# Sums of v on sixteen 32x32 TensorE tiles in four PSUM banks, with dense matmuls moved around each visit, and x and the first weights in larger packets

## The chip, the core and the metric

The kernel runs on one core of one Trainium2 chip. The metric is device time in microseconds of one launch, from the first to the last instruction and what lies around them. A profile is one execution of its own, with its own time beside the span of its instructions.

## What is computed

The reference mixes two branches of a layer over 2048 rows of 512 numbers with a gate per row:

```python
x = A_x
g = _sigmoid((x * gate_w).sum(-1, keepdims=True))
a = jnp.einsum("bsd,ed->bse", x, dft_hid_re);  b = jnp.einsum("bsd,ed->bse", x, dft_hid_im)
A = jnp.einsum("ts,bse->bte", dft_seq_re, a) - jnp.einsum("ts,bse->bte", dft_seq_im, b)
qkv = x @ wqkv                       # 32 heads of 16
scores = q @ k.T * 16 ** -0.5        # each query sees its last 256 keys
B = softmax(scores) @ v @ wo
return g * A + (1 - g) * B
```

Everything is in float32. Nearly all of the arithmetic is in the two 2048x2048 products of the first branch ("the sequence DFT" below); the second branch is a windowed attention.

## The kernel before

**Two streams on one TensorE.** The attention is a loop over 8 groups of four heads times 16 blocks of 128 rows (`n` from 0 to 127, `k = n - 9` for the part that lags behind), in four steps `p` each. The other stream is a Python generator, `dense()`, which emits one dense matmul at each `next`: the projections to q, k and v, the hidden DFT, and after those the sequence DFT (`c_block`, `c_pair`). When the last projection has been emitted, `"proj"` is put into the set `have`. `fill` runs twice in each step `p` and takes 1.95 items of the dense stream each time. Every dense product is made of three float32r terms of split operands (hi times hi, hi times lo, lo times hi); the splitting is done by `hi_of` (ScalarE) and `lo_of` (VectorE or GpSimd).

**A dense item while attention runs** is a pair of matmuls (`mm`, L218): the upper 64 rows of the operands go into one PSUM bank, the lower 64 rows into another, and the two run side by side in the array. "Pair" below means this.

**A step of the attention.** `s_head` (L337) makes a block of scores in PSUM; VectorE reduces it over the keys to the row's bound (L340, a custom operation on tile `sm` with its accumulator read into `nm`). `t_head` (L394) makes the transposed scores of an older block with that bound folded in; ScalarE takes the exponential into the SBUF tile `pt` (L395), and GpSimd zeroes what lies outside the window (L401, L405). Once in four blocks, `m_rows` (L347, L348 and four transposes, L352, all VectorE) turns sixteen columns of bounds into rows for a later block.

**A visit of `pv`.** Once in four blocks, in step `p == 2` between its two `fill` calls, `pv(u)` multiplies the exponentials with v: for each of 4 or 6 blocks of keys (`kb`; 4 when `u` is a multiple of 4), four heads `j` and two halves `h` of 64 rows, one float32 matmul of a 64x32 weight tile of `vpad`, which streams up to 320 columns of `pt`. The two halves add into two PSUM tiles `o`, the four heads into four groups of 32 partitions of each. TensorE then holds eight independent 64x32 tiles. The profile shows a float32 matmul as two passes, so a visit of 6 blocks is 48 instructions and 96 rows. Column 16 of `vpad` is ones, so the sums of the exponentials come along. ScalarE copies the first tile to `os` (L426), VectorE adds the second (L427), and `o_out` stores `os`. There are 32 visits.

**PSUM.** Of the eight banks, four belong to the dense sums. The other four (`ps_a`, tag `st`) are taken in rotation by `s`, `t` and `o` tiles alike. A tile can be written when the operation that reads the bank's former tile is done.

**Order.** Nothing is rearranged after the Python code has run: each engine executes its instructions in the order of the calls. `defer(ticks, fn)` puts a call off by a number of ticks of a clock that each dense item and each step moves on; `tick(9)` after `pv` runs what is due in the next nine.

**The start.** `load_x_first(0)` loads the first quarter of x in four transfers of 128x512 on SyncE's queue and the first q and k weights come in four of 128x256 on ScalarE's (L144). `first_w(dk)` and two more calls split one quarter of the weights and of x at a time; `qk_first` multiplies them, quarter 0 unsplit.

Of the kernel before, what the change touches and what calls it, by code (L numbers as in the profile page):

```python
# [35 lines left out]
def fnet_window_mix(ctx: ExitStack, tc: tile.TileContext, xT, x, wqk, wv, wr, wi, cr, ci, wo, gw, out):  # L36
# [40 lines left out]
    def ld(dst, src):  # L77
        nc.sync.dma_start(dst, src)
# [50 lines left out]
    def load_x_first(ss):  # L129
        for j in range(2):  # L130
            raw = pt_tile([P, 1024])
            for c in range(2):
                XRAW[2 * j + c, ss] = raw[:, HALVES[c]]
            if ss:
                ld(raw.rearrange("p (k s) -> p k s", k=2), xT[ss, 2 * j:2 * j + 2].rearrange("k p s -> p k s"))
# [272 lines left out]
    def pv(u, last=False):  # L408
        g, sb = divmod(u, 4)
        ot = [ps_a.tile([P, 512], F32, name="o", tag="st") for _ in range(2)]  # L410
        kbs = range(max(0, 4 * sb - 2), 4 * sb + 4)
        for kb in kbs:
            pt = PT[g * NB + kb]
            v2 = V2[g * 4 + kb // 4][:, kb % 4]
            for j in range(NH):
                for h in range(2):
                    r = slice(64 * h, 64 * h + 64)
                    a = max(kb * P + (64 * h if kb else 0), sb * 512)
                    e = min(kb * P + 64 * h + 320, sb * 512 + 512)
                    nc.tensor.matmul(ot[h][32 * j:32 * j + 32, a - sb * 512:e - sb * 512], v2[r, j],  # L420
                                     pt[r, j, a - kb * P:e - kb * P], start=kb == kbs[0], stop=kb == kbs[-1],
                                     skip_group_check=True)
# [3 lines left out]
        nc.scalar.copy(os, ot[0])  # L426
        defer(3, lambda: nc.vector.tensor_add(os, ot[1], os))  # L427
        hf = g // 4
# [8 lines left out]
        def o_pack():  # L437
            rows_ = us.rearrange("g j r s -> (g j) r s")
            ld(ls[0], rows_[:, 16])
            ld(o_scr[sb][2 * hf:2 * hf + 2].rearrange("a (b d) s -> (a b) d s", d=16), rows_[:, 0:16])  # L440
            defer(d, l_in)
# [303 lines left out]
    def ring_ahead(n):  # L745
        nonlocal loaded
        while loaded < 4 * NS:
# [6 lines left out]
            loaded += 1  # L754

    def fill(n):
        nonlocal quota
# [18 lines left out]
    for n in range(N + LAG + 1):  # L776
# [4 lines left out]
        for p in range(NH):  # L781
# [71 lines left out]
```

## Time and profile before

| | |
|---|---|
| median of 3 runs | 800.89 us (799.94 to 800.99) |
| the profiled execution | 799.78 us, span of its instructions 798.1 us |
| granted TensorE clock, mean | 0.999 |
| busy share of the span | PE 99%, PEld 87%, DVE 63%, ACT 55%, POOL 53% |
| chain that ended last | PE 98%; the L218 matmuls alone 64%, L420 9% |
| L420 (`pv`) | 2816 matmul rows, 74.0 us busy, at 91 us to 699 us of the span |

PE is TensorE's matmuls, PEld its weight loads, DVE VectorE, ACT ScalarE, POOL GpSimd, SP SyncE. In the views, a row has the start and the length in us, the engine, the source line, the operation, the tile written and the tiles read, the shape, the count, and in brackets the idle time of the engine just before and what ended it. Matmuls are pipelined: their rows overlap, and the distance between two starts says more than a row's length.

### The profile page before, as it was taken

The numbers are of one execution on the slowest core, as the hardware profiler recorded it, in microseconds if no ns is written. First come the engines' busy times: TensorE is split into PE (matmuls) and PEld (weight loads), VectorE is DVE, ScalarE is ACT, GpSimd is POOL, SyncE is SP. The second block draws the span as 40 slices with busy tenths as digits, with TensorE's granted clock in tenths as the row PEclk, the third lists the DMA queues.
The fourth block names the chain that finished last, engine by engine and source line by source line (L and its number), as shares of the span: only waits on it lengthen the run. The fifth ranks groups of instructions, "written<-read, shape, count | busy, mean of one in ns | idle before, by whom it ended". The sixth has DMA issues, their size and how long they took to land.

```text
span 798.1 us, 22896 instructions
## 1 busy us (share of the span) xinstructions
PE 792.8 (99%) x8716; PEld 691.6 (87%) x8716; DVE 502.9 (63%) x1529; ACT 436.6 (55%) x892; POOL 421.0 (53%) x690
## 2 busy tenths in 40 slices
PE   9999999999999999999999999999999999999998
PEld 6788899989998998899888888998899988888886
DVE  5388888887887665656665655566756671255542
ACT  6334776667767665655556556565655555422210
POOL 5002666666667676666566666665765667500000
PEclk9999999999999999999999999999999999999999
DMA  7866778886785256657666554997756545578872
GB/s 287 264 170 210 226 258 278 269 275 210 238 259 183 62 150 199 195 147 224 196 168 177 168 139 145 261 295 229 228 171 192 160 151 172 167 244 264 290 224 80
DMA packets 87438, 164.06 MB, mean 206 GB/s; under 512 B 29504, under 2 KB 31456, under 8 KB 87200
## 3 DMA queue, kind: packets, MB, share of 16 engines
q1 hardware_dynamic: 85888, 160.49, 66.0%
q10 hardware_dynamic: 1440, 2.10, 0.7%
q8 instruction: 69, 1.13, 0.7%
q14 instruction: 41, 0.34, 0.2%
HBM read 109.84 MB, written 57.16 MB: 209 GB/s over the span
## 4 chain that ended last, share of the span: by engine, by line
PE 98%; DVE 1%; issue 0%; POOL 0%; POOLq 0%
PE d L218 64%; PE d L214 9%; PE o L420 9%; PE t L214 5%; PE t L394 5%; PE s L337 5%; PE t L127 0%; DVE sm L340 0%; DVE mhl L348 0%; DVE mt L352 0%; DVE mhl L347 0%; DVE lo L87 0%; DVE ev L729 0%; DVE es L226 0%; POOL mask L124 0%
## 5 line engine op out<-in xcount | busy, mean ns | idle before, releaser
L218 PE MATMUL d<-big,hi 64*128 64x512 f32 x2096 | 364.5, 393 | 0.0
L340 DVE CUSTOM_DVE_ANT_0 sm<-s,mask 128x384 f32<-128x384 f32 (+2 forms) x512 | 271.2, 530 | 136.6 <-PE s L337 76.9
L395 ACT ACTIVATE pt<-t 128x384 f32<-128x384 f32 (+2 forms) x512 | 238.2, 471 | 155.9 <-PE t L394 81.6
L218 PEld LDWEIGHTS d<-big,hi 64*128 64x128 f32 x2096 | 218.0, 186 | 21.1 <-issue 1.1
L218 PE MATMUL d<-big,lo 64*128 64x512 f32 x1048 | 223.3, 392 | 0.0
L401 POOL TENSOR_SCALAR_AFFINE_SELECT pt<-pt 128x256 f32<-128x256 f32 x256 | 107.7, 421 | 166.5 <-ACT pt L395 147.9
L87 POOL TENSOR_TENSOR lo<-raw,hi 128x512 fp32r<-128x512 f32 x120 | 155.2, 1304 | 25.8 <-ACT hi L84 25.4
L337 PE MATMUL s<-ring,ring 48*128 48x384 f32 (+2 forms) x512 | 162.6, 326 | 0.3
L394 PE MATMUL t<-ring,ring 50*128 50x384 f32 (+2 forms) x512 | 162.1, 328 | 0.0
L218 PEld LDWEIGHTS d<-big,lo 64*128 64x128 f32 x1048 | 115.0, 186 | 10.5 <-issue 0.2
L218 PE MATMUL d<-hi,big 64*128 64x512 f32 x656 | 119.7, 392 | 0.0
L337 PEld LDWEIGHTS s<-ring,ring 48*128 48x128 f32 x512 | 92.1, 184 | 9.7 <-DVE nm L340 2.2
L394 PEld LDWEIGHTS t<-ring,ring 50*128 50x128 f32 x512 | 91.0, 184 | 6.8 <-DVE nm L340 0.7
L405 POOL TENSOR_SCALAR_AFFINE_SELECT pt<-pt 128x256 f32<-128x256 f32 x224 | 92.9, 415 | 0.0
L84 ACT CAST hi<-raw 128x512 fp32r<-128x512 f32 x146 | 87.5, 616 | 8.5 <-issue 7.6
L87 POOL TENSOR_TENSOR hl<-es,hl 128x512 fp32r<-128x512 f32 x34 | 46.1, 1355 | 72.9 <-ACT hl L84 67.0
L218 PEld LDWEIGHTS d<-hi,big 64*128 64x128 f32 x656 | 75.9, 186 | 6.6 <-DVE es L226 0.4
L420 PEld LDWEIGHTS o<-pt,vpad 64*32 64x32 f32 x2816 | 60.2, 106 | 18.5 <-issue 6.1
L218 PE MATMUL d<-lo,big 64*128 64x512 f32 x328 | 75.8, 393 | 0.0
L420 PE MATMUL o<-pt,vpad 64*32 64x320 f32 (+5 forms) x2816 | 74.0, 348 | 0.0
L223 ACT ACTIVATE es<-d 128x512 f32<-128x512 f32 x69 | 41.3, 598 | 26.0 <-PE d L218 22.9
L426 ACT COPY os<-o 128x512 f32<-128x512 f32 x32 | 18.8, 586 | 64.4 <-PE o L420 64.4
(75 smaller groups left out, 783.2 us busy)
## 6 DMA issues: line engine op xcount, KB each, us to landing
qk_scr<-hl SPq DMA_DIRECT2D x32, 512.0 KB
ring<-qk_scr SPq DMA_DIRECT2D x128, 128.0 KB
raw<-cr SPq DMA_DIRECT2D x32, 512.0 KB
raw<-ci SPq DMA_DIRECT2D x32, 512.0 KB
ab_scr<-hl SPq DMA_DIRECT2D x20, 512.0 KB
big<-ab_scr SPq DMA_DIRECT2D x17, 512.0 KB
ring<-qk_scr SPq DMA_DIRECT2D x128, 64.0 KB
u_scr<-os SPq DMA_DIRECT2D x32, 256.0 KB
```

The lines of the kernel that those rows point to most:

```text
L84: nc.scalar.copy(hi, raw)
L87: (nc.gpsimd if pool else nc.vector).tensor_sub(lo, raw, f(hi))
L214: nc.tensor.matmul(pss[0], w, x, start=start, stop=stop)
L218: nc.tensor.matmul(pss[h], w[r], x[r], start=start, stop=stop)
L223: nc.scalar.activation(t, pss[0], AF.Copy, scale=scale)
L337: nc.tensor.matmul(ps[:, :w], ring[0][r, p, jb * P:(jb + 1) * P], ring[1][r, p, k0:k0 + w], start=True, stop=True)
L340: nc.vector.tensor_tensor_reduce(out=sm[:, :w], in0=ps[:, :w], in1=mask[:, WIN - w:], scale=1.0, scalar=3e38, op0=OP.add, op1=OP.min, accu ...
L394: nc.tensor.matmul(ps[:, :w], ring[1][r, p, q0:q0 + P], ring[0][r, p, q0:q0 + w], start=True, stop=True)
L395: nc.scalar.activation(pt[:, j, :w], ps[:, :w], AF.Exp, scale=-1.0)
L401: nc.gpsimd.affine_select(a, a, pattern=[[0, 2], [1, P]], compare_op=OP.is_ge, fill=0.0, base=0, channel_multiplier=-1)
L405: nc.gpsimd.affine_select(a, a, pattern=[[0, 2], [-1, P]], compare_op=OP.is_gt, fill=0.0, base=0, channel_multiplier=1)
L420: nc.tensor.matmul(ot[h][32 * j:32 * j + 32, a - sb * 512:e - sb * 512], v2[r, j], pt[r, j, a - kb * P:e - kb * P], start=kb == kbs[0], st ...
```

## The change

Three edits.

**Sixteen tiles.** Once `"proj"` is in `have`, `pv` cuts the 128 rows into four parts of 32 instead of two of 64. Each part streams 288 columns at most instead of 320, into an `o` tile of its own, so a visit takes four PSUM tiles and 96 instructions (64 when there are 4 blocks) instead of two tiles and 48 (32). ScalarE copies the first tile, and VectorE adds three instead of one, each into `os`; the store follows 16 ticks after instead of 7. In the built program this holds for the last 22 of the 32 visits: 17 of 6 blocks and 5 of 4.

**Dense items moved.** Around such a visit `borrow` takes three items of the dense stream just ahead of `pv` and five just behind it. `fill` pays the eight back over the next 32 calls, a quarter of an item each, so that it takes 1.7 in a call in place of 1.95. The number of dense matmuls is the same (4664 at L218 and L214, counting each of a pair).

**Larger packets.** The host lays x out so that two quarters of the contraction stand side by side: the first x comes in two transfers of 128x1024 instead of four of 128x512 (and the others contiguous), the first weights in two of 128x512 instead of four of 128x256.

```diff
     def load_x_first(ss):
...
-            if ss:
-                ld(raw.rearrange("p (k s) -> p k s", k=2), xT[ss, 2 * j:2 * j + 2].rearrange("k p s -> p k s"))
-            else:
-                for c in range(2):
-                    ld(raw[:, HALVES[c]], xT[ss, 2 * j + c])
+            ld(raw, xT[ss, j])
...
-    for dk in range(DK):
-        c = slice(dk * 256, dk * 256 + 256)
+    for c in HALVES:
         nc.scalar.dma_start(wqraw[:, c], wqk[0][:, c])
...
     def pv(u, last=False):
-        ot = [ps_a.tile([P, 512], F32, name="o", tag="st") for _ in range(2)]
+        rows_ = 32 if "proj" in have else 64
+        ot = [ps_a.tile([P, 512], F32, name="o", tag="st") for _ in range(P // rows_)]
...
-                for h in range(2):
-                    r = slice(64 * h, 64 * h + 64)
-                    a = max(kb * P + (64 * h if kb else 0), sb * 512)
-                    e = min(kb * P + 64 * h + 320, sb * 512 + 512)
+                for h in range(P // rows_):
+                    r = slice(rows_ * h, rows_ * h + rows_)
+                    a = max(kb * P + (rows_ * h if kb else 0), sb * 512)
+                    e = min(kb * P + rows_ * h + 256 + rows_, sb * 512 + 512)
...
         nc.scalar.copy(os, ot[0])
-        defer(3, lambda: nc.vector.tensor_add(os, ot[1], os))
+        for h in range(1, P // rows_):
+            defer(3 * h, nc.vector.tensor_add, os, ot[h], os)
...
-        defer(7, o_out)
+        defer(7 if rows_ == 64 else 16, o_out)
...
+    def borrow(n):
+        nonlocal debt
+        debt += n
+        for _ in range(n):
+            next(stream, None)
     def fill(n):
...
-        quota += rate / 2
+        pay = min(debt, 0.25)
+        debt -= pay
+        quota += rate / 2 - pay
...
+                    wide = "proj" in have
+                    if wide:
+                        borrow(3)
                     pv(k // 4 - 1)
                     tick(9)
+                    if wide:
+                        borrow(5)
                     v_ahead(k // 4 + 1)
```

Lines of the kernel after stand a few lines off: L213 is the pair of L218, L332 and L389 the heads of L337 and L394, L416 the matmul of L420, L335 the reduction of L340, L342 to L347 those of `m_rows`, L75 the adds of L427 (they are called from `tick`).

TensorE's order at the twentieth visit (464 us in the trace of before), from the last `t` head ahead of it to the first matmuls of `pv`. Names are tiles (`d` the dense sums), the sizes those of the moving operand, and the brackets the engines whose semaphores the instruction waits for. Before:

```order
L394 MATMUL t<-ring_261,ring_262 128x384 [waits Activation_49]
L218 MATMUL d_8414<-big,hi 128x512
L218 MATMUL d_8415<-big,hi 128x512
L218 MATMUL d_8414<-big,lo 128x512
L218 MATMUL d_8415<-big,lo 128x512
L420 MATMUL o<-pt,vpad_271 32x64 [waits DVE_49]
L420 MATMUL o<-pt,vpad_271 32x128 [waits Activation_49]
L420 MATMUL o<-pt,vpad_271 32x64
```

Two pairs stand between, and the two `o` tiles wait for the readers of the two banks taken longest ago. The same place after:

```order
L389 MATMUL t<-ring_257,ring_258 128x384 [waits Activation_49]
L213 MATMUL d_8831<-big,lo 128x512
L213 MATMUL d_8832<-big,lo 128x512
L213 MATMUL d_8831<-big,hi 128x512
L213 MATMUL d_8832<-big,hi 128x512
L213 MATMUL d_8831<-big,hi 128x512
L213 MATMUL d_8832<-big,hi 128x512
L213 MATMUL d_8831<-big,lo 128x512 [waits Pool_49]
L213 MATMUL d_8832<-big,lo 128x512
L416 MATMUL o<-pt,vpad_267 32x32 [waits DVE_49]
L416 MATMUL o<-pt,vpad_267 32x64 [waits Activation_49]
L416 MATMUL o<-pt,vpad_267 32x96 [waits DVE_49]
```

Now four pairs stand between (five at other visits), and the third matmul of `pv` waits for VectorE a second time: it writes the bank of the `s` tile made in this same step.

VectorE's order there, from the reduction of step `p == 1` to the add behind the visit. Before:

```order
L340 ISA sm,nm<-s,mask 128x384 [waits DVE_49,PE_49]
L340 ISA nm 128x1
L347 TENSOR_SCALAR mhl<-nm 128x16
L348 SCALAR_TENSOR_TENSOR mhl<-nm,mhl 128x16 [waits DVE_49]
L352 STREAM_TRANSPOSE mt<-mhl 32x32 [waits DMAHW5_49,DVE_49]
L352 STREAM_TRANSPOSE mt<-mhl 32x32 x3
L340 ISA sm,nm<-s,mask 128x384 [waits PE_49]
L340 ISA nm 128x1
L427 TENSOR_TENSOR os<-o,os 128x512 [waits DMAHW7_49,PE_49,Activation_49]
L340 ISA sm,nm<-s,mask 128x384 [waits PE_49]
```

And after:

```order
L335 ISA sm,nm<-s,mask 128x384 [waits DVE_49,PE_49]
L335 ISA nm 128x1
L342 TENSOR_SCALAR mhl<-nm 128x16
L343 SCALAR_TENSOR_TENSOR mhl<-nm,mhl 128x16 [waits DVE_49]
L347 STREAM_TRANSPOSE mt<-mhl 32x32 [waits DMAHW1_49,DVE_49]
L347 STREAM_TRANSPOSE mt<-mhl 32x32 x3
L335 ISA sm,nm<-s,mask 128x384 [waits PE_49]
L335 ISA nm 128x1
L75 TENSOR_TENSOR os<-o,os 128x512 [waits DMAHW6_49,PE_49,Activation_49]
L75 TENSOR_TENSOR os<-o,os 128x512 [waits DVE_49,PE_49] x2
L335 ISA sm,nm<-s,mask 128x384 [waits PE_49]
```

In both, `m_rows` stands between the reductions of steps 1 and 2; after, three adds in place of one stand ahead of the reduction of step 3. On TensorE seven pairs (six at some visits) follow the visit before the heads of step 3, in place of two, and then three or four in each step in place of four.

More of the change, by code (lines that the diff above doesn't have):

```diff
@@ L133, in load_x_first @@
                 XRAW[2 * j + c, ss] = raw[:, HALVES[c]]
-            if ss:
-                ld(raw.rearrange("p (k s) -> p k s", k=2), xT[ss, 2 * j:2 * j + 2].rearrange("k p s -> p k s"))
-            else:
-                for c in range(2):
-                    ld(raw[:, HALVES[c]], xT[ss, 2 * j + c])
+            ld(raw, xT[ss, j])
     wqraw = pt_tile([P, 1024])
     wq0 = [st.tile([P, 1024], F32R, name=h) for h in ("hi", "lo")]
-    for dk in range(DK):
-        c = slice(dk * 256, dk * 256 + 256)
+    for c in HALVES:
         nc.scalar.dma_start(wqraw[:, c], wqk[0][:, c])
@@ L437, in o_pack @@
         def o_pack():
-            rows_ = us.rearrange("g j r s -> (g j) r s")
-            ld(ls[0], rows_[:, 16])
-            ld(o_scr[sb][2 * hf:2 * hf + 2].rearrange("a (b d) s -> (a b) d s", d=16), rows_[:, 0:16])
+            ur = us.rearrange("g j r s -> (g j) r s")
+            ld(ls[0], ur[:, 16])
+            ld(o_scr[sb][2 * hf:2 * hf + 2].rearrange("a (b d) s -> (a b) d s", d=16), ur[:, 0:16])
             defer(d, l_in)
@@ L754, in ring_ahead @@
             loaded += 1
+    debt = 0.0
+    def borrow(n):
[3 more added lines that the diff above has]
+            next(stream, None)
     def fill(n):
-        nonlocal quota
+        nonlocal quota, debt
         rate = FILL_FIRST if n < LAG else FILL_SEQ if "proj" in have else FILL_PROJ
-        quota += rate / 2
+        pay = min(debt, 0.25)
+        debt -= pay
+        quota += rate / 2 - pay
         while quota >= 1:
@@ L832 @@
     arrays = {
-        "xT": x.T.reshape(DK, P, 4, 512).transpose(2, 0, 1, 3),
+        "xT": x.T.reshape(2, 2, P, 4, 512).transpose(3, 0, 2, 1, 4).reshape(4, 2, P, 1024),
         "x": x.reshape(16, P, D),
```

## The prediction

> **What bounds the kernel now.** The page comes first: which engine is full, and which engine the last chain runs through.
>
> ```profile
> span 798.1 us, 22896 instructions
> PE 792.8 (99%) x8716; PEld 691.6 (87%) x8716; DVE 502.9 (63%) x1529; ACT 436.6 (55%) x892; POOL 421.0 (53%) x690
> PE 98%; DVE 1%; issue 0%; POOL 0%; POOLq 0%
> PE d L218 64%; PE d L214 9%; PE o L420 9%; PE t L214 5%; PE t L394 5%; PE s L337 5%; PE t L127 0%; DVE sm L340 0%; DVE mhl L348 0%; DVE mt L352 0%; DVE mhl L347 0%; DVE lo L87 0%; DVE ev L729 0%; DVE es L226 0%; POOL mask L124 0%
> ```
>
> TensorE is the bound from end to end. Whatever shortens its matmuls is gained in full, and whatever makes it wait is lost in full. The number of dense matmuls does not change, so moving them costs nothing by itself, but neither can they hide a wait: each is used once. Next, the chain in order of time gives the length of a visit of `pv`, here one of 6 blocks and the next one of 4:
>
> ```profile
> 464.00 0.47 PE d L218 x4
> 464.47 2.32 PE o L420 x65
> 466.80 0.68 PE d L218 x4
> ...
> 484.43 1.88 PE o L420 x54
> ```
>
> Then the timeline of that first visit, which is one of the 22 that change (u = 19). TensorE:
>
> ```profile
> 462.56 0.34 PE L394 MATMUL t<-ring,ring 50*128 50x384 f32 x1
> 462.57 0.34 PE L337 MATMUL s<-ring,ring 48*128 48x384 f32 x1
> 462.74 0.63 PE L218 MATMUL d<-big,hi 64*128 64x512 f32 x4
> 463.21 0.39 PE L218 MATMUL d<-big,lo 64*128 64x512 f32 x2
> 463.44 0.39 PE L218 MATMUL d<-big,hi 64*128 64x512 f32 x2
> 463.67 0.34 PE L337 MATMUL s<-ring,ring 48*128 48x384 f32 x1
> ...
> 463.84 0.40 PE L218 MATMUL d<-big,hi 64*128 64x512 f32 x2
> 464.07 0.40 PE L218 MATMUL d<-big,lo 64*128 64x512 f32 x2
> 464.40 2.42 PE L420 MATMUL o<-pt,vpad 64*32 64x64 f32 x96
> 466.75 0.73 PE L218 MATMUL d<-big,hi 64*128 64x512 f32 x4
> 467.32 0.34 PE L394 MATMUL t<-ring,ring 50*128 50x384 f32 x1
> ```
>
> The starts tell the prices: a pair takes 0.23 us (463.84 to 464.07), the two heads of a step together 0.17 (462.57 to 462.74). Into the visit the distance is 0.33 instead of 0.23, and the two pairs behind it take 0.57 instead of 0.46: 0.1 us at each end, which I read as the array changing its tiles. There is no other hole. VectorE meanwhile:
>
> ```profile
> 462.94 0.56 DVE L340 CUSTOM_DVE_ANT_0 sm<-s,mask 128x384 f32<-128x384 f32 x1 [0.31 <-PE s L337]
> 463.42 0.08 DVE L340 DVE_READ_ACCUMULATOR2_ANT nm<- 128x1 f32 x1
> 463.42 0.17 DVE L347 TENSOR_SCALAR mhl<-nm 128x16 fp32r<-128x16 f32 x1
> 463.63 0.34 DVE L348 SCALAR_TENSOR_TENSOR mhl<-nm,mhl 128x16 fp32r<-128x16 f32 x1
> 464.00 0.84 DVE L352 STREAM_TRANSPOSE mt<-mhl 32x32 f32<-32x32 f32 x4
> 464.87 0.56 DVE L340 CUSTOM_DVE_ANT_0 sm<-s,mask 128x384 f32<-128x384 f32 x1
> 465.36 0.08 DVE L340 DVE_READ_ACCUMULATOR2_ANT nm<- 128x1 f32 x1
> 467.51 0.69 DVE L427 TENSOR_TENSOR os<-o,os 128x512 f32<-128x512 f32 x1 [2.08 <-ACT os L426]
> ```
>
> This is the view that decides. The `s` made at 463.67 is read only by the reduction that ends at 465.44, because `m_rows` stands ahead of it. Before, nobody minds: the visit at 464.40 takes the banks of the older heads.
>
> **The change part by part. Shorter streams.** In a visit of 6 blocks each half streams 64+192+320+320+256+128 = 1280 columns, by the bounds in the code; each quarter after streams 32+160+288+288+256+128 = 1152. With 4 blocks it is 1024 and 960. The two visits above differ by 256 columns and 0.44 us, 1.7 ns a column, so the change saves up to 0.22 us in each of 17 visits and 0.11 in each of 5: 4.3 us. That is the upper end. The other end is the number of matmuls, which doubles: 2.32 us for 96 rows is 24 ns a row, 1.88 us for 64 is 29. A bound by rows would make both equal; columns fit better (1280 to 1024 is 1.25, the times 1.23, the rows 1.5). No trace here shows sixteen tiles. The chain waits inside the visit (below), so the first rounds start without instructions queued ahead; I take half of the saving, -2.2 us, with -4.3 and +8 (0.36 us a visit lost) as ends inside the forecast, and the full doubling as a rival.
>
> "TensorE: Matmul & The Clock Gate" of the Trainium skill, in "Wait — 56ns, not 53.3ns?", states that matmuls never start closer than about 25 ns, however small. By it 192 rows would need 4.8 us, 2.5 more than the visit now, and the sum would be about 49 us higher; the 24 ns a row of the visit here already lie just under that floor, so the trace does not bear it out across tiles.
>
> **The wait ahead of the visit.** Four `o` tiles need all four rotating banks, so the third one needs the bank of the `s` made in the same step. From the heads of step 1 (462.57) to the end of that reduction (465.44) are 2.87 us. TensorE has, from the same heads, two heads' time and eight pairs in all but one of the 19 visits that still have an `s` (u = 10 to 28): the 1.83 us to 464.40 hold six pairs, two more make 2.30. Wake-up takes 0.03, as from the copy's end below to the add. So this visit, a clean one, waits 0.60 us. How typical is it? Grouped over those 19 visits:
>
> ```profile
> L340 DVE CUSTOM_DVE_ANT_0 sm<-s,mask 128x384 f32<-128x384 f32 (+2 forms) x290 | 154.8, 534 | 103.6 <-PE s L337 61.1 <-PE t L394 37.4
> L352 DVE STREAM_TRANSPOSE mt<-mhl 32x32 f32<-32x32 f32 x76 | 15.2, 200 | 1.4
> L348 DVE SCALAR_TENSOR_TENSOR mhl<-nm,mhl 128x16 fp32r<-128x16 f32 x19 | 8.2, 431 | 0.6
> L347 DVE TENSOR_SCALAR mhl<-nm 128x16 fp32r<-128x16 f32 x19 | 6.6, 346 | 0.0
> ```
>
> L347 and L348 are on average 0.17 and 0.09 us longer than in the clean visit, since a few are like this one, ahead of the visit at 642.5:
>
> ```profile
> 641.42 1.31 DVE L347 TENSOR_SCALAR mhl<-nm 128x16 fp32r<-128x16 f32 x1
> 642.77 0.32 DVE L348 SCALAR_TENSOR_TENSOR mhl<-nm,mhl 128x16 fp32r<-128x16 f32 x1
> ```
>
> That makes 0.87 us a visit; an occasional operation in front of step 1's reduction adds a little. I take 0.90, 19 x 0.90 = +17.1 us. While TensorE waits, the 0.1 us of entry passes too: -1.9. The ends: 0.60 everywhere (11.4), and 1.2 (22.8). Queued behind the waiting matmul is everything on TensorE, so nothing covers it; the three items borrowed ahead of the visit are counted in the 2.30 already. The last three visits have no `s` and do not wait.
>
> **The wait behind the visit.** ScalarE copies, then VectorE adds three times into one tile, each add after the last:
>
> ```profile
> 466.90 0.58 ACT L426 COPY os<-o 128x512 f32<-128x512 f32 x1 [1.83 <-PE o L420]
> 467.73 0.49 ACT L395 ACTIVATE pt<-t 128x384 f32<-128x384 f32 x1 [0.25 <-PE s L337]
> ```
>
> The add starts at 467.51 and takes 0.69; with 0.03 between them the second ends at 468.92, the third at 469.64. TensorE goes on at 466.75: seven pairs (0.34 + 6 x 0.23) bring it to the heads of step 3 at 468.5, when the first add is done; 0.17 and three pairs later, at 469.36, the next `t` needs the bank of the third add: 0.31 us of wait. 15 of the 19 visits have ten pairs there, four have eleven (0.08): 15 x 0.31 + 4 x 0.08 = +5.0 us, ends 2 and 7. After that the reduction of step 3, queued behind the adds, is done 0.6 later, well before its bank is wanted, so the delay ends there.
>
> **The start.**
>
> ```profile
> 5.01 1.88 PE L214 MATMUL d<-pt 128*128 128x512 f32 x4
> ...
> 5.47 0.41 ACT L84 CAST hi<-pt 128x256 fp32r<-128x256 f32 x1 [1.49 <-DMA pt<-wqk]
> ...
> 6.49 0.41 ACT L84 CAST hi<-pt 128x256 fp32r<-128x256 f32 x1
> ...
> 7.55 0.41 ACT L84 CAST hi<-pt 128x256 fp32r<-128x256 f32 x1
> ```
>
> The splits of weight quarters 1, 2 and 3 begin at 5.47, 6.49 and 7.55, about as the quarters land. In halves, quarter 1 lands no later, but quarter 2 comes with quarter 3, up to 1.06 late; against that fewer issues stand on ScalarE's queue. Ends -0.5 and +1.1, I take +0.2, since TensorE has 2 us of quarters 0 and 1 in hand. Later x loads and the store that follows 16 ticks after the visit wait for nobody on the chain.
>
> **Sum.** Profiled execution 799.78 (span 798.1 and 1.7 around it) - 2.2 + 17.1 - 1.9 + 5.0 + 0.2 = 818.0. The median of the three runs, 800.89, lies 1.1 above the profiled one, so the forecast is **819**. Its own range: 800.9 - 4.3 + 11.4 - 1.9 + 2 - 0.5 = 807.6, and 800.9 + 8 + 22.8 - 1.9 + 7 + 1.1 = 838, hardly all at once, say 836.
>
> **The rivals.** *The waits are covered and only the shorter streams count*: 800.9 - 4.3 + 0.2 = 797. It decides from the point where the reduction of step 2 ends within 2.30 us of step 1's heads. For it: ScalarE's side is in time. Against it: 2.87 in a clean visit, and `m_rows` keeps its place in VectorE's order in all 19. Chance 0.09. *The number of matmuls binds*: every visit doubles, 17 x 2.32 + 5 x 1.88 = +49 us without the waits, 850, up to 870 with them. Against it: columns fit the two lengths, rows do not. Chance 0.08. *The waits are half as long as I think*, because VectorE, idle for 2.08 us in the visit, carries less backlog in the new rhythm: 800 to 807. Chance 0.07.
>
> **How the numbers follow.** The forecast has 0.76. Its range, widened to 805 for the half-long waits and to 840 for a partial cost of the doubled rows, holds about 8 in 10. 0.2% (1.6 us) is about what a measurement of this kernel can tell from no change. Faster by more: 0.09, the covered case. Within it: 0.02, out of the third rival. Slower: 0.89.
>
> **What would show it.** Right: in the waits of the profile after, TensorE's loads of the `o` matmuls wait for VectorE's `nm` (L335) by some 0.6 to 1 us at visits 10 to 28 and not at the last three; the heads after a visit wait for the adds (L75) by 0.3; PE's busy share falls to about 97%. Wrong: no idle time ahead of L416 (the first rival), or visits of over 4 us with no wait in them (the second). A first dense matmul far from 5.0 us would make the start's term wrong.

## The result and the profile after

The changed kernel takes 874.44 us (median of 6 runs, 872.98 to 877.28) against 800.94 (6 runs on the same chip): 1.092 times as long, 95% interval 1.090 to 1.094. The forecast was 819, 805 to 840: the sign is right, the size is not. The span of its instructions is 74.8 us longer than before (798.1).

The head of the page of the changed kernel, and its line of the queue that brings instructions (packets, MB, share):

```profile
span 872.9 us, 26875 instructions
PE 839.9 (96%) x10668; PEld 732.5 (84%) x10668; DVE 530.4 (61%) x1571; ACT 435.3 (50%) x892; POOL 423.1 (48%) x692
q8 instruction: 84, 1.38, 0.7%
```

Of the kernel before, the same line:

```profile
q8 instruction: 69, 1.13, 0.7%
```

TensorE has 1952 more rows (976 float32 matmuls, two rows each), is busy 47 us longer and idle 28 us longer. Fifteen more packets of 16.4 KB have come. The waits of the weight loads of after (what waited, for what, us in total, times, longest):

```profile
PEld o L416 <- issue: 20.0, 29, 3.3
PEld o L416 <- DVE nm L335: 15.4, 20, 1.5
PEld d L213 <- issue: 8.0, 11, 3.3
PEld t L389 <- DVE os L75: 6.2, 14, 0.6
PEld s L332 <- DVE nm L335: 3.1, 9, 0.6
```

Two of these waits were forecast: `o` for `nm`, and `t` for `os`. The largest was not: TensorE waits at the `o` matmuls for nothing that the profile shows ("issue"), up to 3.3 us at a time. The timeline of TensorE at the visit that the prediction showed at 464.40, now at 503.31:

```profile
503.31 0.30 PE L416 MATMUL o<-pt,vpad 32*32 32x32 f32 x4
503.97 3.59 PE L416 MATMUL o<-pt,vpad 32*32 32x96 f32 x188 [0.35 <-DVE nm L335]
507.49 0.73 PE L213 MATMUL d<-big,hi 64*128 64x512 f32 x4
```

VectorE there:

```profile
503.35 0.56 DVE L335 CUSTOM_DVE_ANT_0 sm<-s,mask 128x384 f32<-128x384 f32 x1
503.83 0.08 DVE L335 DVE_READ_ACCUMULATOR2_ANT nm<- 128x1 f32 x1
508.22 2.28 DVE L75 TENSOR_TENSOR os<-o,os 128x512 f32<-128x512 f32 x3 [4.30 <-ACT os L422]
```

After four rows TensorE waits until the reduction of step 2 is done (503.91), as forecast: 0.57 us between the starts of the fourth row and the fifth, which is the first of the third matmul. But then 188 rows take 3.5 us where 96 took 2.3 in all. In some visits there is a hole as well, a stretch in which TensorE stands idle and the profile shows nothing that it waits for. Here, from 456 us on, it is 2.73 us in the middle of the `o` matmuls:

```profile
453.29 3.18 PE L416 MATMUL o<-pt,vpad 32*32 32x96 f32 x159 [0.67 <-DVE nm L335]
459.20 0.48 PE L416 MATMUL o<-pt,vpad 32*32 32x96 f32 x29 [2.73 <-issue]
```

The start, TensorE's first dense matmuls and ScalarE's splits of weight quarters 1 and 2:

```profile
5.89 2.68 PE L209 MATMUL d<-pt 128*128 128x512 f32 x4 [0.41 <-DMA pt<-wqk]
5.87 0.41 ACT L84 CAST hi<-pt 128x256 fp32r<-128x256 f32 x1 [2.85 <-DMA pt<-wqk]
8.01 0.40 ACT L84 CAST hi<-pt 128x256 fp32r<-128x256 f32 x1 [1.22 <-DMA pt<-wqk]
```

Summed over the trace from the starts of the rows (a visit without its waits is the time from its first to its last start, less every distance over 0.25 us):

| part | forecast | measured, us |
|---|---|---|
| start, up to the first visit | +0.2 | +1.5 |
| 22 visits without waits: 2.18 to 3.41 (6 blocks), 1.68 to 2.49 (4) | -2.2 | about +23 |
| wait ahead of the third matmul, 19 visits (and 0.26 ahead of the second in five) | +17.1 - 1.9 | +14.9 (and +1.3) |
| holes inside visits, six of 1.0 to 3.3 | none | +12.5 |
| between visits: three holes of 3.4, 2.2 and 1.5, the waits behind the visit, and a halved clock | +5.0 | +22 |

The halved clock stands in no line of the forecast. The granted TensorE clock, 0.999 in the execution before, is 0.990 in this one: the trace grants half of it in four stretches of 3.4 or 6.8 us, 17 us in all, which begin at 297.45, 413.50, 485.19 and 645.61 us, each in or up to 1.6 us behind a hole of over 2 us between two starts. (Behind a fifth such hole, the one at 456, the clock stays.) Behind the first of the three holes between visits a pair of dense matmuls takes 0.42 us in place of 0.23:

```profile
298.14 1.22 PE L213 MATMUL d<-big,hi 64*128 64x512 f32 x4 [3.11 <-issue]
299.17 0.63 PE L213 MATMUL d<-big,lo 64*128 64x512 f32 x2
299.59 1.05 PE L213 MATMUL d<-big,hi 64*128 64x512 f32 x4
```

The four intervals between visits in which this happens lost some 5 us more than four clean ones, their holes taken out.

### The profile page after: what moved, and what is told of

Same layout as the page of the kernel before. It is cut to its first block, busy times and chain, and to the rows that moved or that the text cites. A ratio compares the mean times of both kernels' runs of the same rounds, so it can differ in the third digit from the quotient of the medians.

```text
span 872.9 us, 26875 instructions
## 1 busy us (share of the span) xinstructions
PE 839.9 (96%) x10668; PEld 732.5 (84%) x10668; DVE 530.4 (61%) x1571; ACT 435.3 (50%) x892; POOL 423.1 (48%) x692
## 5 line engine op out<-in xcount | busy, mean ns | idle before, releaser
L213 PE MATMUL d<-big,hi 64*128 64x512 f32 x2096 | 391.9, 399 | 4.2 <-issue 4.2
L335 DVE CUSTOM_DVE_ANT_0 sm<-s,mask 128x384 f32<-128x384 f32 (+2 forms) x512 | 271.4, 530 | 122.5 <-PE s L332 79.0
L213 PEld LDWEIGHTS d<-big,hi 64*128 64x128 f32 x2096 | 256.6, 189 | 21.7 <-issue 5.7
L213 PE MATMUL d<-big,lo 64*128 64x512 f32 x1048 | 253.4, 397 | 1.7 <-issue 1.7
L87 POOL TENSOR_TENSOR lo<-raw,hi 128x512 fp32r<-128x512 f32 x122 | 157.9, 1303 | 76.3 <-ACT hi L84 76.1
L389 PE MATMUL t<-ring,ring 50*128 50x384 f32 (+2 forms) x512 | 165.1, 333 | 1.4 <-DVE os L75 0.2
L332 PE MATMUL s<-ring,ring 48*128 48x384 f32 (+2 forms) x512 | 163.9, 329 | 0.2
L213 PEld LDWEIGHTS d<-big,lo 64*128 64x128 f32 x1048 | 142.5, 188 | 10.0 <-issue 1.9
L416 PE MATMUL o<-pt,vpad 32*32 32x288 f32 (+15 forms) x4768 | 105.7, 339 | 20.2 <-issue 10.2
L75 DVE TENSOR_TENSOR os<-o,os 128x512 f32<-128x512 f32 x76 | 52.6, 692 | 117.0 <-ACT os L422 112.3
L416 PEld LDWEIGHTS o<-pt,vpad 32*32 32x32 f32 (+1 forms) x4768 | 81.5, 103 | 49.1 <-issue 20.0
L213 PE MATMUL d<-hi,big 64*128 64x512 f32 x656 | 120.4, 392 | 0.0
L389 PEld LDWEIGHTS t<-ring,ring 50*128 50x128 f32 x512 | 92.1, 186 | 11.7 <-DVE os L75 6.2
L332 PEld LDWEIGHTS s<-ring,ring 48*128 48x128 f32 x512 | 93.4, 187 | 9.0 <-DVE nm L335 3.1
L213 PEld LDWEIGHTS d<-hi,big 64*128 64x128 f32 x656 | 76.9, 186 | 5.9 <-DVE es L221 0.4
L213 PE MATMUL d<-lo,big 64*128 64x512 f32 x328 | 77.0, 393 | 0.0
```

The source lines that it names most:

```text
L75: fn(*args)
L87: (nc.gpsimd if pool else nc.vector).tensor_sub(lo, raw, f(hi))
L213: nc.tensor.matmul(pss[h], w[r], x[r], start=start, stop=stop)
L332: nc.tensor.matmul(ps[:, :w], ring[0][r, p, jb * P:(jb + 1) * P], ring[1][r, p, k0:k0 + w], start=True, stop=True)
L335: nc.vector.tensor_tensor_reduce(out=sm[:, :w], in0=ps[:, :w], in1=mask[:, WIN - w:], scale=1.0, scalar=3e38, op0=OP.add, op1=OP.min, accu ...
L389: nc.tensor.matmul(ps[:, :w], ring[1][r, p, q0:q0 + P], ring[0][r, p, q0:q0 + w], start=True, stop=True)
```

## The experiments

My theory after the result: the doubled matmuls bind, each float32 matmul costing 33 ns (3.2 us over 96), and the holes are instructions that come too late. The rivals: the moved dense matmuls or the larger packets cost it; columns or weights cost it; the holes are waits for data. Times are medians beside the kernel before on the same chip (799.8 to 800.9).

### One part at a time

**The larger packets alone** (the loads of x and of the first weights, and the host's layout of x, on the kernel before).

> The kernel before with the larger packets alone. If the packets are what moved the first visit from 91.2 to 92.7 us of the span, this run is 1.5 us slower than before (802.4), with the first dense matmul near 5.9 us and the split of weight quarter 2 near 8.0. If that shift came from elsewhere, it is within 0.3 us of before.

801.42 us, ratio 1.0015 (1.0006 to 1.0023), 1.2 us: nearer to the first value than to the second. The first dense matmuls and the split of quarter 2 come 0.41 and 1.36 later than before:

```profile
5.42 2.15 PE L209 MATMUL d<-pt 128*128 128x512 f32 x4
7.85 0.41 ACT L84 CAST hi<-pt 128x256 fp32r<-128x256 f32 x1 [1.53 <-DMA pt<-wqk]
```

**The moved dense matmuls alone** (`borrow(3)` and `borrow(5)` around the old `pv`, `fill` paying back).

> The kernel before with the dense items moved (three ahead of and five behind each of the last 22 visits, paid back a quarter at a time), but eight tiles and two banks as before. Theory one, that moving dense items costs nothing by itself: within 1 us of before (800 to 802). Rival, that the new rhythm itself delays the heads or the instruction supply: 5 us or more slower, with idle time between the visits.

801.3 us, ratio 1.0009 (1.0000 to 1.0018): moving them costs next to nothing where nothing waits.

**The tiles without the moved matmuls.** Both calls taken out of the changed kernel:

```diff
-                    if wide:
-                        borrow(3)
                     pv(k // 4 - 1)
                     tick(9)
-                    if wide:
-                        borrow(5)
```

> The changed kernel with the dense matmuls left where they were before (none taken ahead of or behind a visit): the sixteen tiles and the larger packets alone. If the moved matmuls hide waits one for one, three of them (0.70 us) come back as a wait ahead of the third row in the 19 visits that waited there, +13 us, and five (1.16 us) as a wait behind each of 22 visits, up to +25: 895 to 912 us, with the holes at packet boundaries as before. If the waits were covered anyway, 870 to 878.

902.65 us, ratio 1.126 (1.121 to 1.130), in the range for moved matmuls that hide waits one for one. They save 28 us of what the tiles cost: by the starts, 11 us ahead of the third matmuls and 16 between visits. A part of that is the clock, which this trace halves for 31 us, the one of the changed kernel for 17. The waits of the weight loads here:

```profile
PEld o L416 <- DVE nm L335: 26.1, 21, 2.6
PEld o L416 <- issue: 17.3, 25, 2.9
PEld t L389 <- DVE os L75: 15.6, 32, 0.5
PEld s L332 <- ACT os L422: 8.4, 19, 0.5
```

So the sixteen tiles cost all but the 1.2 us of the larger packets, and the moved matmuls give a part of it back.

### The waits, and what is left without them

**Nine matmuls ahead in place of three.**

```diff
-                        borrow(3)
+                        borrow(9)
...
-        pay = min(debt, 0.25)
+        pay = min(debt, 14 / 32)
```

> The kernel after with nine dense items ahead of the visit instead of three (paid back 14/32 of an item in each call). If the third matmul of a visit waits for the reduction of the same step's scores, six more pairs (1.4 us) cover it: the waits ahead of visits, 14.9 us in the trace of after, fall to 1 or 2, and the time to about 861. If TensorE waits there for something that moves along with it, such as its own instructions, the time stays at 873 to 875.

866.13 us, ratio 1.081 (1.079 to 1.084), where about 861 was expected. The wait for `nm` falls from 15.4 to 2.6 us, and only 8 us of it are gained: the holes inside visits grow from 12.5 to 17.9, three of the seven in visits that had none.

```profile
PEld o L416 <- issue: 24.5, 26, 4.1
PEld t L389 <- DVE os L75: 8.1, 15, 0.6
PEld s L332 <- DVE nm L335: 4.9, 10, 0.6
PEld d L213 <- issue: 3.3, 10, 0.8
PEld o L416 <- DVE nm L335: 2.6, 8, 0.4
```

**The five matmuls taken in the middle of the visit.**

```diff
         for kb in kbs:
+            if rows_ == 32 and kb == kbs[len(kbs) // 2]:
+                borrow(5)
```

and the call of `borrow(5)` behind the visit taken out.

> The changed kernel with the five dense matmuls taken into the middle of a visit (ahead of the row of half its blocks) instead of behind it; three stay ahead. If the holes inside visits are the instruction fetch falling behind a burst of 384 instructions, bursts of 192 with five dense matmuls (1.1 us for 10 instructions) between them let it catch up: holes inside visits 12.5 to under 4, the front waits shorter too where the third row lies behind the dense work (no: that is row three, ahead of the middle, so they stay), the wait for the copy behind the visit longer by 0.3 to 0.6 in 22 visits (+7 to +13), two more switches of the array a visit (+0.1 to 0.2 each, +4). About 870 us (862 to 880). If holes have another cause (a wait for PSUM or for exp), they stay and the time rises to 880 to 890.

896.57 us, ratio 1.119 (1.116 to 1.121), above both ranges. Six holes stay inside visits, 0.5 to 2.4 us, 8.5 in sum: the pause of ten dense matmuls, 1.2 us, did not do away with them. And with nothing behind the visit the next heads wait: starts that fell together before lie some 0.7 us apart, and often 0.6 once more, behind nearly every visit.

**The boundaries of the packets moved.** Behind the warm-up matmuls of the changed kernel:

```diff
+    for _ in range(32):
+        nc.tensor.matmul(ps[:32, :8], mask[:32, :32], mask[:32, :8], start=True, stop=True)
```

> The changed kernel with 32 float32 matmuls of 32 x 32 by 8 columns more at the very start, behind the three of the warm-up, where PE waits for the first load: 128 instructions of 64 B, half a packet of 256. If the holes inside visits lie on the boundaries of instruction packets, every boundary moves by half a packet against the program: the holes (visits 15, 17, 22, 23, 25, 30 in the changed kernel) leave these places and turn up at others, their sum 5 to 22 us, and the time moves with that sum: 865 to 884 us. If they come from the data (a tile that is late, a bank that is not free), they stay in the same visits with the same lengths and the time stays at 874 to 876.

874.57 us, the same time, and every hole inside a visit is elsewhere: visits 15, 17, 22, 23, 25 and 30 have none left, seven new ones stand in 11, 13, 19, 21, 27, 29 and 31, 14.8 us in sum. The visit whose hole was shown above, and a new one, on TensorE:

```profile
455.29 3.57 PE L418 MATMUL o<-pt,vpad 32*32 32x96 f32 x188 [0.67 <-DVE nm L337]
...
500.09 3.19 PE L418 MATMUL o<-pt,vpad 32*32 32x96 f32 x159 [0.35 <-DVE nm L337]
506.14 0.71 PE L418 MATMUL o<-pt,vpad 32*32 32x96 f32 x29 [2.86 <-issue]
```

The data are the same; what differs is the place of each instruction in its packet, and a start that is 4.8 us longer. The holes go with the packets. The three holes between visits are gone as well (one of 1.8 us stands behind visit 14), and the intervals there lose 6 us less; that this makes up for the longer start, so that the time is the same, is luck.

### What a matmul costs

**Twice the count on the old tiles.** In the last 22 visits of the kernel before, each `pv` matmul in two halves of its columns, one right behind the other:

```diff
-                    nc.tensor.matmul(ot[h][..., a - sb * 512:e - sb * 512], v2[r, j],
-                                     pt[r, j, a - kb * P:e - kb * P], ...
+                    cuts = (a, (a + e) // 2, e) if "proj" in have else (a, e)
+                    for i, (a, e) in enumerate(zip(cuts, cuts[1:])):
+                        nc.tensor.matmul(ot[h][..., a - sb * 512:e - sb * 512], v2[r, j],
+                                         pt[r, j, a - kb * P:e - kb * P], ...
```

> The kernel before, but in the last 22 visits each float32 matmul of pv is cut into two of half the columns: eight tiles, two banks, one add and the same columns as before, and the number of matmuls of the kernel after. Theory one, that a visit is bound by how fast TensorE gets its instructions (96 matmuls at 33 ns, 3.2 us, and holes when the supply runs dry): visits of 3.3 to 3.5 us (64 matmuls: 2.4 to 2.6), no wait for VectorE ahead of them, some holes of 1 to 3 us; 825 to 848 in all. Theory two, that sixteen small tiles in four banks are slow in themselves: visits of 2.2 to 2.4 us and 801 to 806 in all.

842.29 us, ratio 1.052 (1.051 to 1.054). Visits of 3.43 and 2.55 us without holes, 15 us of holes, 84 instruction packets: the same visits as with sixteen tiles. One without a hole, and the dense matmul behind it:

```profile
461.12 3.62 PE L422 MATMUL o<-pt,vpad 64*32 64x32 f32 x192
464.67 0.50 PE L218 MATMUL d<-big,hi 64*128 64x512 f32 x2
```

The holes stand in the six visits in which the changed kernel has them and in two more (14 and 19), though tiles, banks and waits are those of the kernel before: one more sign that they go with the place in the program and not with the data. The length of the visits I took as proof of a fixed price of a matmul; the next runs took that back.

**bfloat16.** The tiles of `PT` and `vpad` declared in bfloat16, on the changed kernel and on the one before.

> The changed kernel with exp(scores) and v of the pv matmuls kept in bfloat16 instead of float32 (8 bits of mantissa: a lower precision, not the reference's). A float32 matmul was fed as four instructions, a bfloat16 one as two; the number of matmuls (96 or 64 a visit in the last 22 visits) and their columns stay. If instructions bind at 8.3 ns each: a visit of 96 takes 96 x 16.7 ns + 0.2 = 1.8 us instead of 3.4, one of 64 about 1.3 instead of 2.5; 192 instructions a visit are less than one 16 KB packet, so the holes of 1 to 4 us inside visits (12.5 us) nearly go; q8 falls from 84 packets to about 47. With the first ten visits (-1 us each) about -35 - 12 - 10 = 57 less: 815 us (800 to 830), the waits for VectorE ahead of a visit still there. If what binds is one matmul per 33 ns whatever its instructions: visits stay at 3.2 us and the time at 860 to 872. If the columns bound: visits fall below 1 us and the time to 795 or less.

797.95 us, ratio 0.996 (0.995 to 0.998). The visits take 0.81 and 0.60 us, no hole is left, the wait for `nm` stays:

```profile
385.79 1.00 PE L416 MATMUL o<-pt,vpad 32*32 32x96 bf16 x94 [0.44 <-DVE nm L335]
```

That is 8.4 ns a matmul (0.81 us over 96), a quarter of the 35.5 in float32 (3.41 over 96), with half of the instructions. Visits of 1.8 us were expected if each instruction costs 8.3 ns, so that is wrong too, and the time lies in none of the three ranges.

> The kernel before (64 rows a tile, eight tiles, 48 matmuls a visit of 192 rows) with exp(scores) and v of the pv matmuls in bfloat16 (a lower precision, not the reference's). Instructions bind: 48 x 16.7 + 0.2 = 1.0 us a visit instead of 2.18, 32 visits, some of it lost again to PE waiting for the copies of the banks: -37 + up to 12, 763 to 777 us. One matmul per 33 ns: 1.6 + 0.2 = 1.8 us a visit, 790 us. Either way the 16 tiles of the changed kernel in the same precision come out slower than this.

776.33 us, ratio 0.970 (0.968 to 0.972): the fastest version here, where that precision is enough. The time lies in the first range, but by luck: the visits take 0.55 us and not 1.0. They are some 49 us shorter in all and the time is 24: most of the rest comes back as TensorE's wait for the reductions, here in the kernel before

```profile
PEld s L337 <- DVE nm L340: 2.2, 6, 0.5
```

and here in bfloat16 (a single wait of 5.4 us at 540 us, for a load of `ring`, is another part):

```profile
PEld s L337 <- DVE nm L340: 24.9, 29, 2.2
```

**Narrower weights.** In the changed kernel:

```diff
+                    m = 17 if rows_ == 32 and kb == 4 * sb + 3 else 32
-                    nc.tensor.matmul(ot[h][32 * j:32 * j + 32, ...], v2[r, j],
+                    nc.tensor.matmul(ot[h][32 * j:32 * j + m, ...], v2[r, j, :m],
```

> The changed kernel with the weights of the last key block of each wide visit (16 of 96 or of 64 matmuls) cut from 32 columns to 17 (16 of v and the column of ones, the others only repeat it): same result, same number of instructions. If the 33.3 ns of a float32 matmul go with the columns of its weights (the load of the weights), these 16 take 17.7 ns each: 0.25 us less in each of 22 visits, 5.5 us, 868 to 870. If they are a fixed price of a float32 matmul, whatever its tile, the visits keep 3.41 and 2.49 us and the time stays at 873 to 876.

873.6 us, ratio 1.090 (1.086 to 1.094); the visits keep 3.40 and 2.48 us, where 0.25 us less was expected if the weights' columns counted. They are not it.

**The price by itself.** 96 small matmuls of each kind at the start (`feed`: loops over tile positions, 8 columns).

> The kernel before with five rows of 96 small matmuls (8 columns of zeros each) at the very start, to measure the disputed price by itself: float32 with weights of 32 rows by 32 columns on sixteen tiles; float32 32 by 16; float32 64 by 32 on eight tiles; bfloat16 32 by 32; bfloat16 32 by 16. They leave the rest of the kernel as it was, some 10 us later. A fixed price of a float32 matmul: 33 ns for each of the first three, 3.2 us a row, and 8.4 ns for both in bfloat16, 0.8 us. A price that goes with the columns of the weights: 33, 17, 33, 8.4, 4.2 ns. A price that goes with rows by columns of the weights: 33, 17, 67, 8.4, 4.2 ns. Where a packet of 256 instructions ends inside a float32 row (384 instructions in 3.2 us), a hole of 1 to 3 us.

TensorE's timeline (one execution; its time, 825.3 us, is only the longer start):

```profile
5.41 2.20 PE L136 MATMUL o<-mask 32*32 32x8 f32 x217
12.40 1.23 PE L136 MATMUL o<-mask 32*16 32x8 f32 x128 [4.80 <-issue]
16.41 1.45 PE L136 MATMUL o<-mask 32*16 32x8 f32 x128 [2.78 <-issue]
20.14 1.16 PE L136 MATMUL o<-mask 64*32 64x8 f32 x103 [2.28 <-issue]
21.22 0.26 PE L136 MATMUL o<-half 32*32 32x8 bf16 x25
23.86 1.16 PE L136 MATMUL o<-half 32*32 32x8 bf16 x128 [2.38 <-issue]
```

Two readings. A float32 matmul of 8 columns costs 20 ns (217 rows, two to a matmul, in 2.20 us), not 33: there is no fixed price of 33, and for float32 all three expectations missed (in bfloat16, 128 rows in 1.16 us are 9 ns a matmul, near the 8.4 of the first). And the matmuls come in bursts of 128 rows in both types. With a weight load to each row that is 256 instructions, and 16.4 KB over 256 is 64 bytes: a burst is a packet. Once the packets fetched ahead are used up, a packet lasts 1.2 to 1.5 us and the next comes 2.3 to 2.8 us later (4.8 the first time): some 3.7 us from one packet's start to the next, also from 16.41 us on, when hardly any other transfer runs.

**Rounds over the tiles.** Behind seven dense float32 matmuls each (time for the fetch), rounds of small matmuls over chosen tiles and with more columns.

> The kernel before with eight rows of small matmuls on zeros at the very start, each behind seven dense float32 ones of 128 x 128 by 384 (4 us in which the instructions catch up): float32 on sixteen tiles with 256, 128 and 32 columns; on the four tiles of one column group (248 columns); on the four tiles of one row group (240 columns); on eight tiles of 64 rows with 256 and 128 columns; bfloat16 on sixteen tiles with 128. The wide visits took 586 to 673 ns for a round over the sixteen tiles, the 427 to 480 of the longest stream (1.67 ns a column) and more. If the sixteen tiles are independent and only the count binds, at the 20 ns of the row of 8 columns: a round of sixteen takes 427, 320 and 320 ns, the rounds of four 414 and 400, those of eight 427 and 214. If a float32 matmul has a fixed price of 33 ns: 533, 533, 533 for sixteen, 414 and 400 for four, 427 and 267 for eight. If the four tiles above one another share their way out (0.58 ns a column, from 670 ns for 4 x 288 columns): about 600, 300, 300 for sixteen, 575 for four in one column group and 400 for four in one row group. If the four side by side share their way in: the same with the two swapped. bfloat16: 16 x 8.4 = 135 ns a round.

One execution; three of its rows (96 rows are three rounds over sixteen tiles, or six over eight):

```profile
10.05 2.13 PE L140 MATMUL o<-mask 32*32 32x256 f32 x96
16.82 1.49 PE L140 MATMUL o<-mask 32*32 32x128 f32 x96
49.83 2.82 PE L140 MATMUL o<-mask 64*32 64x256 f32 x96
```

From the starts of rows, in the second round and later (for sixteen tiles that is two rounds): sixteen tiles 649 ns with 256 columns, about 450 with 128, 283 to 307 with 32; eight tiles 432 and 218; four in one column of the array, which write four banks, 418 (248 columns), four in one row 405 (240). Four and eight tiles take just their stream, 1.69 ns a column. Sixteen take more than the stream and more than the count at 20 ns a matmul (320), so neither a shared way in or out nor a fixed price fits. Sixteen bfloat16 tiles with 128 columns take 133 ns, as expected from the visits (135), and their rows start 8 to 9 ns apart all along: there a price of 8.3 ns a matmul does fit. In float32, what fits is that not all sixteen work at once: 16 x 432 / 649 is 10.7 tiles on the average. A limit on the matmuls under way would also explain the halves in a row, with which four or five of eight tiles would hold them all. The next two runs were made for that.

**The halves taken apart.** As with twice the count, but the eight first halves of a key block ahead of its eight second halves:

```diff
+            for i in range(2 if "proj" in have else 1):
                 for j in range(NH):
                     for h in range(2):
...
+                        a, e = cuts[i:i + 2]
```

> The kernel before with each pv matmul of the last 22 visits cut into two halves of its columns, as in the run with twice the count, but with all first halves of a key block's eight tiles ahead of all second halves, so that no tile gets two matmuls in a row. The same 96 or 64 matmuls and the same instructions. If some 20 rows (ten float32 matmuls, each two rows) can be under way at once, the eight tiles with two rows each all work again: visits of 96 at 2.2 to 2.5 us instead of 3.43, of 64 at 1.7 to 1.9 instead of 2.55, holes at the packet boundaries as long or longer (15 to 25 us): 815 to 835 us instead of 842. If a float32 matmul has a fixed price of 33 ns, the visits keep 3.4 and 2.5 us and the time 838 to 848.

838.06 us, ratio 1.049 (1.042 to 1.055). The same instructions in another order, and the visits without holes take 2.62 and 1.98 us instead of 3.43 and 2.55 (2.2 to 2.5 and 1.7 to 1.9 expected). The time is only 4 us less, which the two intervals do not tell from nothing, and lies 3 over its range: the visits without holes are 17 us shorter in all, but the holes inside visits grow from 15 to 19 us and the intervals between visits by 6. A visit without a hole on TensorE, 2.77 us to the next dense matmul:

```profile
463.10 2.84 PE L423 MATMUL o<-pt,vpad 64*32 64x32 f32 x192
465.87 0.50 PE L218 MATMUL d<-big,hi 64*128 64x512 f32 x2
```

So in float32 the price is not one of the count alone.

**The limit by itself.**

> The kernel before with seven rows of small float32 matmuls on zeros at the start, each behind seven dense ones, to see how many tiles work at once. A round of sixteen with 256 columns took 649 ns where one stream takes 427: 10.5 tiles at work on the average; with 128 columns 450 and 213: 7.6; eight tiles with 128 or 256 columns all worked. If the number under way is limited to about ten matmuls (20 rows): sixteen with 352 columns 860 to 900 ns a round; twelve tiles with 256 about 490; ten with 248 about 415 to 440; eight of 32 rows with 256 about 430, like eight of 64 rows; eight tiles with two matmuls of 128 in a row 600 to 650 for the round of sixteen matmuls instead of 2 x 218 = 436; eight with 64 columns 148 (18.4 ns each); sixteen with 64 columns 300 to 350. If sixteen small tiles are slow because of their 32 rows: eight of 32 rows also take 550 or more, and the two in a row take 436. If the excess is 220 ns for every round whatever its tiles: eight of 32 rows 650.

One execution; rows for twelve tiles, ten, eight of 32 rows, and eight with two matmuls in a row:

```profile
17.77 2.35 PE L138 MATMUL o<-mask 32*32 32x256 f32 x96
24.76 2.52 PE L138 MATMUL o<-mask 32*32 32x248 f32 x100
31.93 2.82 PE L138 MATMUL o<-mask 32*32 32x256 f32 x96
39.39 2.09 PE L138 MATMUL o<-mask 64*32 64x128 f32 x96
```

Rounds from the starts: eight tiles of 32 rows 432 ns, as of 64 rows; ten 418 to 443 (248 columns); twelve 456 to 464 (490 expected); sixteen with 352 columns 744 to 790; two of 128 in a row on eight tiles 669 to 695 instead of 436 (twice 218). Tiles at work, at 1.69 ns a column: 8, 10, 11, 12 and 5 (ten matmuls, two to a tile). So small tiles are not slow, and with long streams some ten to twelve float32 matmuls are under way at once. The sixteen with 352 columns came out faster than expected and the two in a row slower, so the number is not sharp; with 128 and 64 columns (450; 327 to 358) only 8 and 5 of sixteen tiles work, though 18 ns a matmul would allow more. The starts show a change of pace besides: in the rounds on sixteen tiles the first 30 or so rows start 7 ns apart, the later ones, with 256 and 352 columns, mostly 17. A price of 17 ns a row alone would make every round of sixteen 544 ns, more than was measured with 128 columns and less than with 256, so it is not the whole either. What sets the limit stays open.

The Trainium skill, in "TensorE: Matmul & The Clock Gate", under "Architectural detail: the array is 16× 32×32, not 1× 128×128", gives TensorE a queue of 64 instructions. One round of sixteen float32 matmuls at four instructions each would be 64; the rounds with 256 columns here fill only two thirds of the tiles. The 30 or so rows that start fast, 60 instructions with their loads, would fit such a queue, but no run shows the queue itself. Under "The mechanism" that page of the Trainium skill gives tiles side by side one stream and about 4 ns more for each further tile. By that, as an estimate, a round of sixteen with 256 columns would take 492 ns (432 + 15 x 4), and 649 were measured.

## Why the prediction was wrong, point by point

**Shorter streams: the step that failed.** "1.7 ns a column" was right for eight tiles, which all work, and the two lengths of visit could only show that. For sixteen tiles I let it stand, because "columns fit the two lengths, rows do not". A round over sixteen tiles takes some 220 ns more than its stream (649 for 432), a visit of six blocks 1.23 us more where I had 0.11 less, and the visits +23 us in all where I had -2.2. The largest part has the wrong sign; the sum has the right one because of the waits. The end I gave, 0.36 us a visit, was a third of it. The rival *the number of matmuls binds* named the right term and about the right total (850 to 870, at 0.08), by a wrong reason: doubling the visit would give 4.6 us, the visits take 3.41, and the same count in a good order 2.62. The floor of about 25 ns, from the Trainium skill ("TensorE: Matmul & The Clock Gate", "Wait — 56ns, not 53.3ns?"), would give 4.8 us, as an estimate; rows stood 18 ns apart in the visits and 10 in the small test. What keeps the sixteen tiles from working all at once stays open.

**The instruction packets: a term that was not there.** The profile of before had the line, 69 packets. A visit of 96 float32 matmuls is 384 instructions, one and a half packets, used up in 3.4 us. Where two boundaries fall into one visit (the six holes lie at rows 132 to 163 of 192, so another boundary lies 128 rows ahead of each) TensorE waits 1 to 3.3 us. That is +12.5 us inside visits and some 7 behind them, and the halved clock behind four of the holes adds some 5. The run with the boundaries moved showed that the holes go with the packets. With nine matmuls ahead, 8 us were gained in place of 13; that a visit which starts sooner waits longer for its packet fits this, but its boundaries had moved too.

**The wait ahead of the visit: right.** 0.57 us in the visit shown (0.60 forecast), +14.9 in all against +15.2, for the reduction of step 2 behind `m_rows`, and none in the last three visits. Nine matmuls ahead took it away.

**The wait behind the visit: right place, undersized.** The three adds come one after the other (2.28 us, 2.13 forecast), and the `t` of the next head waits for the third. A clean interval between visits lost some 0.6 us, not 0.31 and 0.08; with small holes in it, about +15 in all in place of +5 (at most 7). Some 5 of the 15 go with the halved clock. How much of the other 10 is the adds and how much late instructions was not taken apart.

**The start: outside its bound.** +1.5 where +1.1 was the end. Quarter 2 was late as feared (8.01 for 6.49), but the loss is there before it is used: the fourth row of the first dense matmuls starts 1.67 us later than before. The first row starts 0.88 later (5.89 for 5.01), and the next ones follow more slowly: 1.01 and 0.64 us after the row ahead, where every distance is 0.43 before. Quarter 1 came 0.40 later here, but not in the run with the packets alone (5.39 for 5.47). Without the larger packets the first visit came up to 1.2 us late as well (the kernel before in bfloat16), so one trace cannot tell how much of the +1.5 is theirs; by eleven runs they cost 1.2 us (0.5 to 1.8).

**The borrowed matmuls at nothing: right** (+0.7 us by themselves). That "neither can they hide a wait" was wrong: left where they were before, they make the changed kernel 28 us slower.

## What to carry to other kernels

Read from a trace how many tiles work at once, as tile count times stream over the time of a round, before cutting a matmul into smaller ones: eight float32 tiles were full here, sixteen gave no more than ten to twelve. Two matmuls in a row to one tile waste the others; go round the tiles first. And count instructions in a burst against the packets that bring them: a burst of 384 in 3.4 us waited in the visits into which two boundaries fell (six of the 17 visits of six blocks here, seven others with the boundaries moved), so fewer and longer matmuls are worth more than balanced ones. Look at the granted clock behind such a hole as well.

## What was not expected of the hardware

Instructions come to TensorE in packets of 256 (16.4 KB), and back to back a packet took 3.7 us, 14 ns an instruction, while TensorE took one in 4.5 ns (128 rows and their loads in 1.16 us). By the counts of packets and rows, a float32 matmul is four instructions and two rows, a bfloat16 one two and one; on sixteen tiles in the visits they cost 35.5 and 8.4 ns (3.41 and 0.81 us over 96).
